# Sparse attention and a softplus layer on one core: values loaded once, fewer small transfers, matmul results in banks of their own

## The chip, the core and the metric

The kernel runs on one core of a Trainium2 chip. A core has five engines that run side by side, each through its own queue in order: TensorE (PE in the profile, its weight loads PEld) multiplies and transposes into PSUM; VectorE (DVE) and ScalarE (ACT) read PSUM and SBUF; GpSimd (POOL) works on SBUF alone; SyncE (SP) issues all the DMAs here. PSUM has eight banks of 512 float32 columns for each of 128 partitions. The metric is the device time of one execution in microseconds: the median of three runs before is 1411.3 us (1410.25 to 1415.76).

## What is computed

```python
def _attn_ref(q, k, v, tau):                      # 8 batches, 8 heads, 576 rows, 64 wide
    scores = 1/sqrt(64) * matmul(q, k^T)
    thresh = max(scores, axis=-1) - tau
    scores = where(scores >= thresh, scores, -1e9)
    attn = exp(scores - max(scores))
    attn = attn / (sum(attn) + 1e-9)
    return matmul(attn, v)

def _moe_ref(x, w_in, w_out):                     # x: 4608 x 512, w_in: 512 x 2048
    h = x @ w_in
    g = maximum(h, 0) + log1p(exp(-abs(h)))       # softplus
    return g @ w_out
```

The attention's output, heads side by side, is x. The output is 4608 x 512 float32.

## The kernel before

**Units and tiles.** A unit is one batch's pair of heads: 8 x 4 = 32 units. Each of the two heads has 576 rows: 512 in four blocks of 128 and a rest of 64. The two rests make one block together, so a unit has nine tiles of 128 query rows: t = 0 to 3 of head 0, t = 4 (`M`) the two rests, t = 5 to 8 of head 1. In SBUF a head's row p x 4 + c lies on partition p in slot c, so that one DMA moves 1 KB runs.

**Per tile.** `scores` multiplies queries by keys into one of two score buffers (`banks`, two PSUM banks each, 288 columns used in each bank). `row_max` (DVE) gives the negated maximum, `exps` (ACT) the exponential into one of three SBUF buffers `e_all` and the threshold, `mask` (DVE) zeroes what lies under the threshold and sums the row. `scores` of tile g + 3 are asked for while tile g is at hand, so they wait for the mask of tile g + 1, which is the last to read that score buffer.

**Whole and split units.** The first eight units (`s.whole`, 72 tiles) keep float32: `whole_T` transposes the exponentials on TensorE, four blocks of 128 into a general PSUM bank (`tm`) and the 64 rest columns into free columns of the tile's score buffer (line 501); ACT copies both (`whole_copy`). The other 24 units split weights and values into float16 halves: `weights_hi` (POOL) writes the upper half of 2^15 e, `weights_lo` (DVE) subtracts it for the lower one, both laid out in nine blocks of 64 columns where upper and lower alternate; a DMA transpose brings them to `eT`, and `values` multiplies nine 128-row blocks of it by the values in `vt`. As each block holds 64 keys' upper halves and the same 64 keys' lower halves, the values of these 64 keys lie on both halves of the partitions: `load_v` loads all values of a split unit twice, with six DMAs. `top_v` finds the largest magnitude of the values for a scale: a DVE maximum per partition, a TensorE product that spreads it over 128 columns into free columns of score buffer 0 (`spare[0]`, line 363), and two points later a maximum over these. `split_v` scales on ACT and splits on POOL, one head at tile 6 and one at tile 8 of the unit before.

**Row scales.** At the end of a unit the reciprocals of the row sums are transposed by TensorE into `spare[1]` (line 595), copied by ACT (`rt`), stored to DRAM (`r_d`), and read back, spread over 64 partitions for each head, by four DMAs into `R` (lines 608 and 609). POOL multiplies the unit's result `xp` by R (line 614); the rest columns then go to DRAM (`x_d`, line 620).

**Queries.** `qkT` transposes keys and queries into general banks; `queries` scales the queries into `qT0` and `swap` writes `qT1`, the same with the two 64-partition halves exchanged, by two DMAs (lines 429 and 430). The block of the two rests, `qm`, is swapped by two more.

**Second layer.** Ten chunks (eight batches' main rows, two sets of rests) go through `hidden` (line 695), `softplus`, the split into `g` (lines 175 and 176) and `project` (line 759). They are interleaved with the attention's tiles by a quota per tile; what is left is done after the last tile.

**Order.** The program is written in the order of the string `PAT`, thirteen different steps per tile with two calls of `point`, and `defer(n, f)` puts f at the n-th point from there. The Tile framework then orders each engine's queue and adds the semaphores; it orders any two accesses of different engines to one PSUM bank. Four general banks (`ps_g`, `GB = 4`) hold transposes, hidden sums, projections and attention results. All helpers' DVE and ACT work shows line 152.

Of the kernel before, what the change touches and what calls it, by code (L numbers as in the profile page):

```python
# [24 lines left out]
P = 128  # L25
# [37 lines left out]
def tile_kernel(ctx: ExitStack, tc: tile.TileContext, q, k, v, tau, w_in, w_out, out):  # L63
# [56 lines left out]
    qm = cpool.tile([P, 2, 2, P], F32R, name="qm")  # L120
# [215 lines left out]
    def load_v(s):  # L336

        if s.whole:
            s.vn = apool.tile([P, 10, D], F32, tag="vt", bufs=2, name=f"vn_{s.i}")
            load_rows(s, s.vn, v)  # L340
            for j in range(2):
                nc.sync.dma_start(
                    s.vn.rearrange("p (h s) d -> p h s d", h=2)[j * SR:(j + 1) * SR, :, NC, :],
                    v[s.b, 2 * s.hp:2 * s.hp + 2, SM:S, :].rearrange("h p d -> p h d"),
                )
            return
        s.vn = apool.tile([P, 2, 9, D], F32, tag="vn", bufs=1, name=f"vn_{s.i}")
        for i in range(2):
            for j in range(2):
                src = v[s.b, 2 * s.hp + j]  # L350
                nc.sync.dma_start(
                    s.vn[i * SR:(i + 1) * SR, j, 1:9, :].rearrange("p (n c) d -> p n (c d)", n=2),
                    src[0:SM, :].rearrange("(n p c) d -> p n (c d)", n=2, c=NC))
            nc.sync.dma_start(s.vn[i * SR:(i + 1) * SR, :, 0, :],
                              v[s.b, 2 * s.hp:2 * s.hp + 2, SM:S, :].rearrange("h p d -> p h d"))

    def top_v(s):
        tops = cpool.tile([P, 1], F32, tag="vtop", bufs=2, name=f"vtop_{s.i}")
        vn = s.vn.rearrange("p s d -> p (s d)" if s.whole else "p h s d -> p (h s d)")
        vec.tensor_reduce(tops, vn, axis=AX.X, op=ALU.max, apply_absolute_value=True)  # L360

        def spread():
            nc.tensor.matmul(spare[0], tops.to_broadcast([P, P]), ident, start=True, stop=True)
            defer(2, take)

        def take():
            top = cpool.tile([P, 1], F32, tag="top", bufs=3, name=f"topv_{s.i}")
            vec.reduce_max(top, spare[0], axis=AX.X)
            to_scale(v_scale[:, s.i:s.i + 1], top)
            ready.add(("v", s.i))  # L370
# [3 lines left out]
    def split_v(s, j):  # L374
        if s.whole:
            return
# [20 lines left out]
    def qkT(s, j, n):  # L397
# [12 lines left out]
        if n == 0:  # L410
            s.kT.append(apool.tile([P, S], F32R, tag="kT", name=f"kT_{s.i}_{j}"))
            t = s.kT[j]
            defer(1, lambda: act.copy(t[:, SR:S], ps))
        else:
            t = [apool.tile([P, SM], F32R, tag=f"qT{i}", name=f"qT{i}_{s.i}_{j}") for i in range(2)]
            s.qT.append(t)
            defer(1, lambda: queries(s, t[0], t[1], ps))

    def queries(s, t0, t1, ps):

        act.activation(t0, ps, AF.Copy, scale=qscale)
        if s.i:
            swap(t0, t1)
# [8 lines left out]
    def qkT_rest(s, j, ps):  # L432

        act.copy(s.kT[j][:, 0:SR], ps[:, j * SR:(j + 1) * SR])
        if j == 0:
# [3 lines left out]
            swap(qm[:, 0], qm[:, 1])  # L439
# [5 lines left out]
    spare = [bank[:, 0, HS:HS + P] for bank in banks]  # L445
    nth = [0]

    def scores(s, t):
        if t == 0:
            s.sums = apool.tile([P, 9], F32, tag="sums", name=f"sums_{s.i}")  # L450
            s.e, s.sp, s.m, s.e16, s.eT, s.bank = {}, {}, {}, {}, {}, {}
# [4 lines left out]
        s.bank[t] = sp  # L456
# [41 lines left out]
    def whole_T(s, t):  # L498
        e = s.e.pop(t)
        main = ps_g.tile([P, NC, P], F32, tag="g", name=f"tm_{s.i}_{t}")  # L500
        rest = s.bank.pop(t)[0:SR, 1, HS:HS + P]
        for c in range(NC):
            nc.tensor.transpose(main[:, c, :], e[:, SR + c * P:SR + (c + 1) * P], ident)
        nc.tensor.transpose(rest, e[:, 0:SR], ident)
# [38 lines left out]
    def weights_hi(s, t):  # L543

        pool, tag, bufs = (apool, "e16", EB) if now["tile"] < TE or t % 2 else (wpool, "wi", WB)
        s.e16[t] = h = pool.tile([P, 9, 2, SR], F16, tag=tag, bufs=bufs, name=f"e16_{s.i}_{t}")
        nc.gpsimd.tensor_scalar(out=h[:, :, 0, :], in0=s.e[t].rearrange("p (c n) -> p c n", n=SR),  # L547
                                scalar1=2.0 ** 15, scalar2=1.0, op0=ALU.mult, op1=ALU.mult)

    def weights_lo(s, t):  # L550
        h = s.e16[t]
        vec.scalar_tensor_tensor(out=h[:, :, 1, :], in0=s.e.pop(t).rearrange("p (c n) -> p c n", n=SR),
                                 scalar=2.0 ** 15, in1=h[:, :, 0, :], op0=ALU.mult, op1=ALU.subtract)

    def weights_T(s, t):
# [3 lines left out]
        h = s.e16.pop(t).rearrange("p c i n -> p (c i n)")  # L559
        if t == M:  # L560
            nc.sync.dma_start_transpose(s.eT[0][:, :, SM:S], h[0:SR])
            nc.sync.dma_start_transpose(s.eT[1][:, :, SM:S], h[SR:P])
# [4 lines left out]
    def values(s, g):  # L567
# [4 lines left out]
        for c in range(9):  # L572
            slot = 0 if c == 0 else 1 + 4 * ((c - 1) % 2) + (c - 1) // 2
            nc.tensor.matmul(o[:, 0:HS], s.vt[:, j, slot, :], s.eT[j][:, c, x0:x0 + HS], start=(c == 0), stop=(c == 8))  # L574
# [23 lines left out]
    def row_scales_out(s):  # L598
# [461 lines left out]
```

## Time and profile before

| | us |
|---|---|
| median of three runs | 1411.3 |
| the profiled execution | 1418.82 |
| its span, first to last instruction | 1417.1 |
| PE busy | 1296.0 |
| DVE / ACT / POOL busy | 919.3 / 920.1 / 943.4 |

The profile counts an engine as busy while one of its instructions runs; matmuls overlap each other, so a busy TensorE is not one at its peak. The whole units fill the first 330 us or so, the split units the stretch to about 1277 us (the last transposed block is multiplied at 1276.5 us), and the rest is the second layer alone. A row "A <- B: x, n, y" of the waits reads: engine and tile A stood idle x us in total, n times, at most y us, until B was done. A row of groups has line, engine, operation, tiles, shapes and count, then busy us and the mean ns of one. A row of one tile's or one line's instructions has minimum, median and maximum ns. The timeline gives start, length, engine, line, operation and, in brackets, the idle time before it with what ended it. A row of stretches has length, then busy us and count for PE, PEld, DVE, ACT and POOL, then the granted clock of TensorE, the mean busy share of 16 DMA engines and GB/s.

### The profile page before, as it was taken

What the parts mean: (1) busy time and instruction counts of PE and PEld (TensorE: products, weight loads), DVE (VectorE), ACT (ScalarE), POOL (GpSimd) and SP (SyncE); (2) the same over time, 40 slices, a digit from 0 to 9 for tenths busy, and PEclk for the clock granted to TensorE, in tenths of its full rate; (3) what the DMA queues carried; (4) which work ended last, traced back from release to release, by engine and by line L of the source; (5) the groups of instructions that cost most, each with busy time, mean ns of one, the idle gap of its engine ahead of it and who ended that gap; (6) DMA issues with size and microseconds to landing.
All of it is one profiled execution on the core that took longest, in us unless ns stands there. A gap on an engine that the chain in (4) does not pass through costs nothing.

```text
span 1417.1 us, 22079 instructions
## 1 busy us (share of the span) xinstructions
PE 1296.0 (91%) x7192; PEld 772.2 (54%) x7192; DVE 919.3 (65%) x1695; ACT 920.1 (65%) x1759; POOL 943.4 (67%) x1033
## 2 busy tenths in 40 slices
PE   6988899899898989899889989898999999999998
PEld 4555555455555555555555555555555765554455
DVE  5878765546777767767777777768667776751011
ACT  5867787766576758665776657666876677753222
POOL 2576876737677778668666777778767778646242
PEclk9998999999999999999999999999999999999999
DMA  5534432213766665656656676766565655631010
GB/s 138 158 108 135 123 99 84 67 38 86 152 127 132 132 146 127 133 129 144 133 131 130 122 153 128 136 123 152 118 133 129 144 115 104 112 77 40 0 38 15
DMA packets 351107, 159.19 MB, mean 112 GB/s; under 512 B 294128, under 2 KB 330256, under 8 KB 350992
## 3 DMA queue, kind: packets, MB, share of 16 engines
q1 hardware_dynamic: 350992, 157.78, 50.4%
q8 instruction: 57, 0.93, 0.3%
q14 instruction: 58, 0.48, 0.1%
HBM read 62.92 MB, written 10.63 MB: 52 GB/s over the span
## 4 chain that ended last, share of the span: by engine, by line
PE 41%; POOL 16%; DVE 13%; ACT 12%; DMA 7%; issue 7%; SPq 4%; POOLq 0%; ACTq 0%; DVEq 0%
PE o L759 12%; PE h L695 12%; PE s L464 6%; PE pv L574 4%; ACT st L152 3%; DVE e L152 3%; PE pv L533 3%; ACT L152 3%; DVE e_all L152 3%; DVE negm L152 3%; DMA R<-r_d 2%; ACT e_all L152 2%; POOL g L176 2%; POOL e L547 2%; POOL q L132 2%
## 5 line engine op out<-in xcount | busy, mean ns | idle before, releaser
L759 PE MATMUL o<-w_o,g 128*128 128x512 f16 x1728 | 422.8, 388 | 14.0 <-POOL g L175 9.6
L695 PE MATMUL h<-xh,w_i 128*128 128x512 f16 (+1 forms) x1280 | 364.4, 361 | 1.8 <-DVE xp L152 1.3
L152 ACT ACTIVATE e_all<-s,negm 128x576 f32<-128x576 f32 x288 | 213.1, 740 | 160.5 <-DVE negm L152 154.0
L152 DVE TENSOR_REDUCE negm<-s 128x1 f32<-128x576 f32 x288 | 215.5, 748 | 135.5 <-PE s L464 102.6
L547 POOL TENSOR_SCALAR e<-e_all 128x576 f16<-128x576 f32 x216 | 202.0, 938 | 149.1 <-DVE e_all L152 140.4
L464 PE MATMUL s<-kT,qT 128*128 128x288 f32 x1024 | 226.5, 342 | 69.8 <-DVE e_all L152 38.9
L152 DVE SCALAR_TENSOR_TENSOR e_all<-s,thr,e_all 128x576 f32<-128x576 f32 x288 | 233.1, 809 | 74.7 <-ACT thr L152 27.3
L695 PEld LDWEIGHTS <-w_i 128*128 128x128 f16 x1920 | 180.3, 99 | 164.6 <-issue 11.3
L759 PEld LDWEIGHTS <-g 128*128 128x128 f16 x1728 | 161.1, 100 | 193.6 <-POOL g L175 16.3
L152 DVE SCALAR_TENSOR_TENSOR e<-e_all,e 128x576 f16<-128x576 f32 x216 | 217.0, 1005 | 36.7 <-POOL e L547 36.6
L695 PE MATMUL h<-xl,w_i 128*128 128x512 f16 (+1 forms) x640 | 231.5, 362 | 2.4 <-POOL xl L176 2.4
L464 PEld LDWEIGHTS s<-kT,qT 128*128 128x128 f32 x1024 | 162.0, 197 | 116.8 <-DVE e_all L152 62.1
L152 DVE SCALAR_TENSOR_TENSOR acc<-o,c,acc 128x512 f32<-128x512 f32 x108 | 80.3, 744 | 181.9 <-PE o L759 121.0
L176 POOL TENSOR_TENSOR g<-st,g 128x512 f16<-128x512 f32 x144 | 168.9, 1177 | 7.5
L175 POOL TENSOR_SCALAR g<-st 128x512 f16<-128x512 f32 x144 | 92.1, 644 | 106.6 <-ACT st L152 106.0
L152 ACT ACT_TABLE_LOAD x119 | 152.7, 1283 | 14.6 <-PE h L695 6.7
L152 ACT ACTIVATE st<-h,c 128x512 f32<-128x512 f32 x144 | 91.1, 683 | 69.2 <-PE h L695 68.4
L574 PE MATMUL pv<-eT,vt 128*128 128x288 f16 x864 | 131.9, 292 | 0.2
L152 ACT COPY xp<-pv 64x288 f32<-64x288 f32 (+3 forms) x136 | 50.8, 378 | 112.1 <-PE pv L574 102.0
L533 PE MATMUL pv<-gw,vn 128*64 128x256 f32 (+3 forms) x320 | 101.2, 437 | 0.0
L614 POOL TENSOR_TENSOR xp<-xp,R 128x576 f32<-128x576 f32 x32 | 46.8, 1463 | 80.8 <-DMA R<-r_d 65.6
L574 PEld LDWEIGHTS <-vt 128*128 128x128 f16 x864 | 79.9, 100 | 34.9 <-issue 2.2
(104 smaller groups left out, 1658.5 us busy)
## 6 DMA issues: line engine op xcount, KB each, us to landing
qT<-qT SPq DMA_DIRECT2D x124, 128.0 KB
vn<-in_v_dram SPq DMA_DIRECT2D x96, 128.0 KB
kn<-in_k_dram SPq DMA_DIRECT2D x32, 256.0 KB
qn<-in_q_dram SPq DMA_DIRECT2D x32, 256.0 KB
wc_i<-in_moe_w_in_dram SPq DMA_DIRECT2D x16, 512.0 KB
R<-r_d SPq DMA_DIRECT2D x64, 128.0 KB
wc_o<-in_moe_w_out_dram SPq DMA_DIRECT2D x16, 512.0 KB
out_dram<-acc SPq DMA_DIRECT2D x32, 256.0 KB
```

The lines of the kernel that those rows point to most:

```text
L132: eng.tensor_tensor(out=out_, in0=in_, in1=hi.bitcast(F32), op=ALU.subtract)
L152: i = getattr(self.eng, name)(*args, **kwargs)
L175: nc.gpsimd.tensor_scalar(out=hi, in0=x, scalar1=1.0, scalar2=1.0, op0=ALU.mult, op1=ALU.mult)
L176: nc.gpsimd.tensor_tensor(out=lo, in0=x, in1=hi, op=ALU.subtract)
L464: nc.tensor.matmul(sp[:, hf, 0:HS], lhs, s.kT[j][:, hf * HS:(hf + 1) * HS], start=(m == 0), stop=(m == len(parts) - 1))
L533: nc.tensor.matmul(o[0:D, 0:n], s.vn[k_, 5 * j + c, :], h[k_, c, 0:n], start=(c == 0), stop=(c == NC))
L547: nc.gpsimd.tensor_scalar(out=h[:, :, 0, :], in0=s.e[t].rearrange("p (c n) -> p c n", n=SR), scalar1=2.0 ** 15, scalar2=1.0, op0=ALU.mult, ...
L574: nc.tensor.matmul(o[:, 0:HS], s.vt[:, j, slot, :], s.eT[j][:, c, x0:x0 + HS], start=(c == 0), stop=(c == 8))
L614: nc.gpsimd.tensor_tensor(out=s.xp, in0=s.xp, in1=s.R, op=ALU.mult)
L695: nc.tensor.matmul(bank[:, i * u.T:(i + 1) * u.T], wi[g, cc][:, a, e], x[cc], start=(cc == 0 and m == 0), stop=(cc == NCC - 1 and m == 2))
L759: nc.tensor.matmul(o, u.g[fc][m // 2][:, sl], wo[fc][:, m % 2, :], start=(n == 0), stop=(n == 3 * QF - 1))
```

## The change

- **Values once.** The weights of a tile are laid out as 576 upper halves, then the lower halves of the last 64 keys, then those of the first 512. After the transposition block c < 4 holds the upper halves of 128 keys, block 4 the upper and the lower halves of the last 64, blocks 5 to 8 the lower halves. Only the last 64 values are needed on both halves of the partitions; the rest is loaded once, by three DMAs, in the layout of the whole units. `split_v` is one step of 640 columns per unit, at tile 7 of the unit before. The keys move from columns 64 to 575 to columns 0 to 511. `weights_lo` becomes two instructions, of 512 and 64 columns.
- **Fewer transfers.** The rests of k and q are loaded by one DMA each, R by two, results of two tiles are stored by one; the queries of head 0 and the block of rests lie in one tile `q0`, swapped together.
- **Banks.** The spread top, the transposed row scales and the transposed rest of whole units go to general banks; the top is taken one point after its product.
- **The ring of g at the end** has ten pairs of buffers where it had eleven, as the tags of the queries hold one buffer each.

```diff
+    q0 = cpool.tile([P, 2, SM + 2 * P], F32R, name="q0")
+    qm = q0[:, :, SM:].rearrange("p n (m c) -> p n m c", m=2)
...
     def natural(s, src, name):
-        for j in range(2):
-            nc.sync.dma_start(t[j * SR:(j + 1) * SR, NC, :], src[s.b, 2 * s.hp + j, SM:S, :])
+        nc.sync.dma_start(t[:, NC, :], src[s.b, 2 * s.hp:2 * s.hp + 2, SM:S, :])
...
     def load_v(s):
+        s.vn = apool.tile([P, 10, D], F32, tag="vt" if s.whole else "vn", bufs=2 if s.whole else 1, name=f"vn_{s.i}")
+        load_rows(s, s.vn, v)
         for i in range(2):
-            for j in range(2):
-                src = v[s.b, 2 * s.hp + j]
-                nc.sync.dma_start(
-                    s.vn[i * SR:(i + 1) * SR, j, 1:9, :].rearrange("p (n c) d -> p n (c d)", n=2),
-                    src[0:SM, :].rearrange("(n p c) d -> p n (c d)", n=2, c=NC))
-            nc.sync.dma_start(s.vn[i * SR:(i + 1) * SR, :, 0, :],
-                              v[s.b, 2 * s.hp:2 * s.hp + 2, SM:S, :].rearrange("h p d -> p h d"))
+            nc.sync.dma_start(
+                s.vn.rearrange("p (h s) d -> p h s d", h=2)[i * SR:(i + 1) * SR, :, NC, :],
+                v[s.b, 2 * s.hp:2 * s.hp + 2, SM:S, :].rearrange("h p d -> p h d"),
+            )
...
         def spread():
-            nc.tensor.matmul(spare[0], tops.to_broadcast([P, P]), ident, start=True, stop=True)
-            defer(2, take)
+            ps = ps_g.tile([P, 512], F32, tag="g", name=f"topv_{s.i}")
+            nc.tensor.matmul(ps[:, 0:P], tops.to_broadcast([P, P]), ident, start=True, stop=True)
+            defer(1, lambda: take(ps))
...
-    def split_v(s, j):
-        if s.whole:
-            return
-        if j == 0:
-            s.vt = apool.tile([P, 2, 9, 2 * D], F16, tag="vt", bufs=2, name=f"vt_{s.i}")
-        vj = s.vn[:, j]
-        act.activation(vj, vj, AF.Copy, scale=v_scale[:, s.i:s.i + 1])
-        halves(s.vt[:, j, :, 0:D], s.vt[:, j, :, D:2 * D], vj)
+    def split_v(s):
+        s.vt = apool.tile([P, 10, 2 * D], F16, tag="vt", bufs=2, name=f"vt_{s.i}")
+        act.activation(s.vn, s.vn, AF.Copy, scale=v_scale[:, s.i:s.i + 1])
+        halves(s.vt[:, :, 0:D], s.vt[:, :, D:2 * D], s.vn)
...
+            if j == 0:
+                t = [q0[:, i, 0:SM] for i in range(2)]
+            else:
+                t = [apool.tile([P, SM], F32R, tag=f"qT{i}", bufs=1, name=f"qT{i}_{s.i}") for i in range(2)]
...
         if s.i:
-            swap(t0, t1)
+            if j == 0:
+                swap(q0[:, 0], q0[:, 1])
+            else:
+                swap(t0, t1)
...
-            swap(qm[:, 0], qm[:, 1])
+            if s.i == 0:
+                swap(qm[:, 0], qm[:, 1])
...
-        rest = s.bank.pop(t)[0:SR, 1, HS:HS + P]
+        rest = ps_g.tile([P, NC, P], F32, tag="g", name=f"tr_{s.i}_{t}")[0:SR, 0, :]
...
-        s.e16[t] = h = pool.tile([P, 9, 2, SR], F16, tag=tag, bufs=bufs, name=f"e16_{s.i}_{t}")
-        nc.gpsimd.tensor_scalar(out=h[:, :, 0, :], in0=s.e[t].rearrange("p (c n) -> p c n", n=SR),
-                                scalar1=2.0 ** 15, scalar2=1.0, op0=ALU.mult, op1=ALU.mult)
+        s.e16[t] = h = pool.tile([P, 2 * S], F16, tag=tag, bufs=bufs, name=f"e16_{s.i}_{t}")
+        nc.gpsimd.tensor_scalar(out=h[:, 0:S], in0=s.e[t], scalar1=2.0 ** 15, scalar2=1.0, op0=ALU.mult, op1=ALU.mult)
...
     def weights_lo(s, t):
-        h = s.e16[t]
-        vec.scalar_tensor_tensor(out=h[:, :, 1, :], in0=s.e.pop(t).rearrange("p (c n) -> p c n", n=SR),
-                                 scalar=2.0 ** 15, in1=h[:, :, 0, :], op0=ALU.mult, op1=ALU.subtract)
+        h, e = s.e16[t], s.e.pop(t)
+        for i, o in ((slice(0, SM), slice(S + SR, 2 * S)), (slice(SM, S), slice(S, S + SR))):
+            vec.scalar_tensor_tensor(out=h[:, o], in0=e[:, i], scalar=2.0 ** 15, in1=h[:, i],
+                                     op0=ALU.mult, op1=ALU.subtract)
...
+        order = (0, 5, 1, 6, 2, 7, 3, 8, 4)
+        for n, c in enumerate(order):
+            nc.tensor.matmul(o[:, 0:HS], s.vt[:, 5 * j + (c if c <= NC else c - NC - 1), :],
+                             s.eT[j][:, c, x0:x0 + HS], start=(n == 0), stop=(n == 8))
...
     def row_scales_T(s):
-        nc.tensor.transpose(spare[1][0:9], s.rs, ident)
-        defer(1, lambda: row_scales_out(s))
+        ps = ps_g.tile([P, 512], F32, tag="g", name=f"rT_{s.i}")
+        nc.tensor.transpose(ps[0:9, 0:P], s.rs, ident)
+        defer(1, lambda: row_scales_out(s, ps))
...
     def load_R(s):
-        for j in range(2):
-            nc.sync.dma_start(s.R[j * D:(j + 1) * D, 0:SM], rows[j * SM:(j + 1) * SM].partition_broadcast(D))
-            nc.sync.dma_start(s.R[j * D:(j + 1) * D, SM:S],
-                              rows[2 * SM + j * SR:2 * SM + (j + 1) * SR].partition_broadcast(D))
+        for a, n in ((0, SM), (2 * SM, SR)):
+            nc.sync.dma_start(s.R[:, a and SM:(a and SM) + n],
+                              rows[a:a + 2 * n].rearrange("(j n) -> j n", j=2)[:, None, :].to_broadcast([2, D, n]))
...
-            spare = [("kT", 2), ("qT0", 2), ("qT1", 2), ("nat", 2), ("e16", EB)]
+            spare = [("kT", "kT", 2), ("qT0", "qT1", 1), ("nat", "nat", 2), ("e16", "e16", EB)]
...
     def store_out(u, tb, a):
         if u.main:
-            dst = out[u.b * S:u.b * S + SM, :].rearrange("(p c) e -> p c e", c=NC)[:, tb, :]
-            nc.sync.dma_start(dst, a)
+            dst = out[u.b * S:u.b * S + SM, :].rearrange("(p c) e -> p c e", c=NC)
+            if u.tail:
+                nc.sync.dma_start(dst[:, tb, :], a)
+            elif tb % 2:
+                nc.sync.dma_start(dst[:, tb - 1:tb + 1, :], u.pairs[tb // 2])
...
-            times = ((s.i - 1, 0), (s.i - 1, 3), (s.i - 1, 6), (s.i - 1, 8))
-        for at_, f in zip(times, (load_v, top_v, lambda x: split_v(x, 0), lambda x: split_v(x, 1))):
+            times = ((s.i - 1, 0), (s.i - 1, 3), (s.i - 1, 7))
+        for at_, f in zip(times, (load_v, top_v, split_v)):
```

More of the change, by code (lines that the diff above doesn't have):

```diff
@@ L412, in qkT, with queries @@
             t = s.kT[j]
-            defer(1, lambda: act.copy(t[:, SR:S], ps))
+            defer(1, lambda: act.copy(t[:, 0:SM], ps))
         else:
-            t = [apool.tile([P, SM], F32R, tag=f"qT{i}", name=f"qT{i}_{s.i}_{j}") for i in range(2)]
+            if j == 0:
+                t = [q0[:, i, 0:SM] for i in range(2)]
+            else:
+                t = [apool.tile([P, SM], F32R, tag=f"qT{i}", bufs=1, name=f"qT{i}_{s.i}") for i in range(2)]
             s.qT.append(t)
-            defer(1, lambda: queries(s, t[0], t[1], ps))
-    def queries(s, t0, t1, ps):
+            defer(1, lambda: queries(s, j, t[0], t[1], ps))
+    def queries(s, j, t0, t1, ps):
         act.activation(t0, ps, AF.Copy, scale=qscale)
         if s.i:
-            swap(t0, t1)
+            if j == 0:
+                swap(q0[:, 0], q0[:, 1])
+            else:
+                swap(t0, t1)
             return
@@ L432, in qkT_rest @@
     def qkT_rest(s, j, ps):
-        act.copy(s.kT[j][:, 0:SR], ps[:, j * SR:(j + 1) * SR])
+        act.copy(s.kT[j][:, SM:S], ps[:, j * SR:(j + 1) * SR])
         if j == 0:
@@ L455, in scores @@
         s.sp[t] = sp
-        s.bank[t] = sp
         if t == M:
```

45 lines of the change are left out of this document (15 added, 30 removed).

## The prediction

> **What bounds the kernel now.** I read the stretches by stage first, then what TensorE waits for, then single episodes in the timeline. One execution is profiled: 1418.82 us, of which the span is 1417.1 us, 7.5 us above the median of 1411.3 us; the sum is made on that execution and its difference then put on the median.
>
> ```profile
> 30.00:180.00 150.00, 128.14 (x683) 82.57 (x681) 120.59 (x248) 110.34 (x276) 104.93 (x111) 0.93 0.46 128
> 180.00:330.00 150.00, 144.48 (x758) 82.08 (x756) 83.19 (x171) 113.63 (x237) 95.11 (x106) 0.99 0.25 68
> 400.00:1000.00 600.00, 541.48 (x3037) 323.90 (x3037) 442.33 (x790) 400.81 (x733) 433.94 (x469) 0.97 0.65 134
> 1000.00:1250.00 250.00, 242.29 (x1450) 149.91 (x1449) 173.97 (x314) 179.30 (x315) 181.86 (x198) 0.99 0.58 122
> core 0: 1417.1 us, clock 0.973
> PE 1296.0 (91%) x7192; PEld 772.2 (54%) x7192; DVE 919.3 (65%) x1695; ACT 920.1 (65%) x1759; POOL 943.4 (67%) x1033
> ```
>
> The columns are the length, then the busy time of PE, PEld, DVE, ACT and POOL, the granted clock, DMA share and GB/s. PE is the bound: 1296.0 of 1417.1 us, so 121 us idle at most to win, and 2.7% of the clock (38 us). The idle time lies from 30 to 180 us (21.9 us) and from 400 to 1000 us (58.5 us); after 1000 us PE is 97% busy. So only those two stages can pay.
>
> ```profile
> PE s L464 <- DVE e_all L152: 39.6, 32, 5.2
> PE s L464 <- DMA qT<-qT: 15.8, 12, 2.2
> PE s L464 <- DVE topv L152: 14.2, 6, 3.7
> PE s L504 <- ACT e_all L152: 12.9, 11, 3.1
> PE o L759 <- POOL g L175: 9.6, 9, 2.2
> POOL xp L614 <- DMA R<-r_d: 65.6, 17, 7.2
> DVE negm L152 <- ACT rt L152: 31.5, 12, 4.4
> DVE e_all L152 <- ACT gw L152: 23.7, 20, 3.3
> DVE e_all L152 <- PE s L363: 12.4, 8, 2.1
> PE tr L409 <- ACT gw L152: 0.6, 2, 0.4
> ```
>
> Each row has us in total, times, longest. Scores wait for the mask that frees their bank (39.6), for swapped queries (15.8), for the values' top, which lies in a score bank (14.2); the short transposes of whole units wait for an exponential that reads the bank they share (12.9). The R wait is POOL's, and one step from PE.
>
> **The change, part by part.** *Results in own banks.* The rows "topv", "L504", "rt", "gw" and "L363" are waits of one bank's users for each other; they go. What is late next is seen in one episode.
>
> ```profile
> 501.93 1.41 POOL L614 TENSOR_TENSOR xp<-xp,R 128x576 f32<-128x576 f32 x1 [1.64 <-DMA R<-r_d]
> 507.01 1.15 DVE L152 SCALAR_TENSOR_TENSOR e<-e_all,e 128x576 f16<-128x576 f32 x1 [3.28 <-POOL e L547]
> 508.09 0.28 DVE L152 TENSOR_REDUCE topv<-s 128x1 f32<-128x128 f32 x1
> 508.42 1.33 PE L464 MATMUL s<-kT,qT 128*128 128x288 f32 x4 [3.66 <-DVE topv L152]
> 602.46 1.47 PE L759 MATMUL o<-w_o,g 128*128 128x512 f16 x6
> 510.46 0.81 DVE L152 SCALAR_TENSOR_TENSOR e_all<-s,thr,e_all 128x576 f32<-128x576 f32 x1
> L152 DVE TENSOR_REDUCE negm<-s 128x1 f32<-128x576 f32 x288 | 215.5, 748 | 135.5 <-PE s L464 102.6 <-ACT rt L152 31.5
> ```
>
> PE stood from 504.76 to 508.42. Without the shared bank it runs these scores, some transposes and six projections (1.47 us where the clock is full) and then needs the mask that now ends at 511.27. That mask stays behind the DVE's work of 507.01, which waited for POOL, which had waited for R; at best the maximum and the mask follow 508.16 directly and end at 509.7 (748 + 810 ns). So 1.5 of 3.66 us stay won: two fifths. I take two fifths for every wait removed, an estimate from this episode.
>
> The top is taken one point (half a tile) sooner. If the DVE comes before PE there, it waits with maxima and masks behind it and PE behind them; the L363 row (12.4 us in 8) is what such waits cost today, and as I count only part of that row as won, nothing more is charged.
>
> *Swaps.* The queries of half 0 and the masked block share a tile: six transfers per unit become four.
>
> ```profile
> 622.97 0.49 SPq L429 DMA_DIRECT2D qm<-qm  x1
> 623.85 0.48 SPq L430 DMA_DIRECT2D qm<-qm  x1
> 624.43 0.55 SPq L429 DMA_DIRECT2D qT<-qT  x1
> 781.39 0.82 PE L464 MATMUL s<-kT,qT 128*128 128x288 f32 x2 [2.05 <-DMA qT<-qT]
> 780.70:787.60 6.90, 6.21 (x21) 3.38 (x22) 3.44 (x6) 3.26 (x7) 6.07 (x8) 0.51 0.65 130
> 787.60:794.50 6.90, 6.90 (x41) 4.11 (x40) 5.83 (x14) 3.11 (x7) 5.69 (x7) 1.00 0.45 86
> ```
>
> The queries go out 1.46 us sooner (624.43 - 622.97), more than the mean wait of 1.3 us (15.8/12); rows grow from 2 to 3 KB, which takes some of it back. The masked block is read four tiles later, so tying it to the queries costs nothing. After the 2.05 us gap PE runs at half clock: 21 matmuls, then 41, in equal stretches. So waits cost twice. The Trainium skill, "TensorE: Matmul & The Clock Gate" (Part 1), has the clock fall after an idle window of some 3.4 us; here 2.05 us did it, so the trace does not agree, and by the page's rule the clock term below would be near zero.
>
> *Values once, R in two, other merges.* Per later unit the values take 3 issues for 6, R 2 for 4, k and q 2 for 3 each: SP issues nine fewer with the swaps. POOL and ACT split 640 columns once where they split 576 twice, at a tile between the two of before; the top is reduced over 640, not 1152. The lower halves become two instructions.
>
> ```profile
> L176 POOL TENSOR_TENSOR vt<-vn,vt 128x576 f16<-128x576 f32 x48 | 62.1, 1293 | 1.3
> L175 POOL TENSOR_SCALAR vt<-vn 128x576 f16<-128x576 f32 x48 | 36.1, 752 | 1.7 <-ACT vn L152 1.6
> L152 DVE TENSOR_REDUCE vtop<-vn 128x1 f32<-128x1152 f32 x24 | 32.4, 1349 | 2.4 <-DMA vn<-in_v_dram 1.0 <-DMA r_d<-rt 1.0
> L152 DVE TENSOR_REDUCE vtop<-vn 128x1 f32<-128x640 f32 x8 | 6.5, 813 | 1.5 <-DMA vn<-in_v_dram 1.5
> L152 DVE SCALAR_TENSOR_TENSOR e<-e_all,e x216: 743/758/1946, 330.0 to 1266.3; 128x576 f16<-128x576 f32 x108
> L152 DVE TENSOR_REDUCE topv<-s x32: 275/278/292, 29.3 to 1218.0; 128x1 f32<-128x128 f32 x32
> L152 DVE TENSOR_SCALAR topv<-topv x32: 136/153/155, 30.3 to 1218.3; 128x1 f32<-128x1 f32 x32
> L608 SPq DMA_DIRECT2D R<-r_d x64: 452/578/603, 56.9 to 1277.4; - x64
> L609 SPq DMA_DIRECT2D R<-r_d x64: 577/592/653, 57.4 to 1278.0; - x64
> L152 ACT COPY gw<-tm 128x512 f32<-128x512 f32 x64 | 37.2, 581 | 15.1 <-PE tm L503 14.8
> 0.00:30.00 30.00, 16.44 (x79) 13.51 (x80) 15.98 (x30) 15.36 (x34) 6.89 (x15) 1.00 0.54 148
> ```
>
> POOL: 2 x (752 + 1293) ns = 4.1 us becomes about 2.3 us (640/576 once), 1.8 us less in each of 24 units; it shortens the queue behind R, of which "POOL g" shows 9.6 us at PE. DVE lower halves: 512 columns lie between 674 ns (758 x 512/576) and 758 ns, 64 columns between 153 and 278 ns; together 827 to 1036 for 758. I take 920, as a line from 153 at one column to 758 at 576 gives 690 + 220: 0.16 us x 216 = 35 us more DVE, less 24 x 0.54 = 13 us of shorter reduces: 22 us. The mask on the same queue frees the banks, so I charge a third, 7 us; the bounds are 0 and 22.
>
> R: two issues fewer send it off 1.17 us sooner (578 + 592 ns); twice the bytes in each lands later. At the stage's 134 GB/s 256 KB take 1.0 us more than 128 KB, so I take nothing; the bad end is the third rival.
>
> PSUM: 72 rests, 32 tops and 32 row scales become 136 more users of the four general banks. PE waits for those banks' readers hardly at all (0.6 us in the row "tr"), the lower bound is 0, and less where a result is read sooner; were each to hold PE up for one copy of 581 ns it would be 79 us. From 180 to 330 us the hidden, value and transposed results are all there at once, so I take a tenth, 8 us. Merged stores, the ring one pair shorter at the end and the values' new order touch no wait shown: 0 (stores lie beside PE; cover gone, half a us each).
>
> **Sum.** Waits removed: 14.2 + 12.9 + 15.8 + 9.6 = 52.5 us, and a quarter of 39.6 for the DVE's rt, gw and L363 waits: 62.4 us; two fifths is 25 us. Clock: 38 us x 52.5/121 = 16 us, two fifths is 6 us. Against it 7 + 8 = 15 us. Net 16 us: the profiled 1418.8 to 1403, on the median 1411.3 to **1395 us**. Own range 1380 to 1407.
>
> **Rivals.**
> 1. *The waits do not come back.* Three quarters are kept: 47 + 12 - 15 = 44 us, 1367 us. For it: POOL's and DVE's relief in the same units. Against: the episode above.
> 2. *No change, 1411 us.* The chain R, POOL, lower halves, mask sets the pace of a unit, and PE's gaps only move. For it: 65.6 us of R waits stay.
> 3. *R becomes slower, and the kernel with it.* The new source of R counts first over the two heads and then 64 equal rows. If the transfer is dealt out by that first count, two DMA engines carry 128 KB each and one 16 KB more. In the first 30 us an engine moves 148/(16 x 0.54) = 17 GB/s, so 8.5 us for 1.1 on sixteen: R lands up to 6 us later. POOL's R waits average 3.9 us (65.6/17); taking the longest, 7.2, to stand behind the longest "POOL g" wait, 2.2, some 5 us are covered, 1.1 are left, and the smaller split gives 1.8. Of 6 us, 3 reach PE, of 4 us 1: at 2.2 in 17 units 38 us more, less the 16: 1433 us. It decides from R landing about 4 us later than now. For it: R is late now already; against: no row shows a transfer so dealt out.
>
> The Trainium skill, "DMA: Bandwidth & Descriptors" (Rules for kernel authors), says an outermost count below 16, a leading broadcast for one, confines a transfer to that many engines. By that page's 435 GB/s for sixteen, one engine would need 4.8 us for 128 KB. No run here shows it.
>
> 4. *Banks run out* from 30 to 330 us, 30 us instead of 8: 1417 us.
>
> **Chances.** Forecast 0.33, rival 1 0.14, rival 2 0.14, rival 3 0.34, rival 4 0.05. Both signs hold much, so the range goes from 1368 (leaving half of rival 1) to 1437 us. A measurement tells 0.5% (7 us) from no change. Faster: the forecast but its edge (0.31), rival 1 (0.14) and 0.03 of rival 3, together 0.48. Within 0.5%: rival 2, most of rival 4 and edges of the forecast and rival 3, 0.20. Slower: the rest, 0.32.
>
> **What would show it.** Right: the topv, rt and L504 rows gone, "PE s <- DVE e_all" above 39.6 us, the qT row below 8 us, POOL's vt near 2.3 us per unit, the lower halves at two pieces of some 0.92 us together. Rival 3: "POOL xp <- DMA R" above 100 us instead of near 50. Rival 4: PE idle above 6 us from 180 to 330 us. Wrong above all if the compiler's order of POOL's queue around R differs, since all the rest waits behind it.

## The result, and the profile after

The changed kernel takes 1516.2 us (median of four runs, 1513.2 to 1520.8), the kernel before 1413.4 us in the same session: 1.072 times the time, 95% interval 1.070 to 1.075. The forecast was 1395, its range 1368 to 1437: the time lies beyond the range, on the slower side, and 83 us beyond the rival of that side. Of the page of the changed kernel the span, the busy times and the chain that ended last by line:

```profile
span 1515.3 us, 21809 instructions
...
PE 1326.3 (88%) x7192; PEld 784.1 (52%) x7192; DVE 990.6 (65%) x1911; ACT 903.0 (60%) x1735; POOL 886.5 (59%) x985
...
PE o L750 11%; DMA R<-r_d 9%; PE h L686 9%; PE s L454 6%; DVE e L153 5%; DVE e_all L153 4%; PE pv L564 4%; DMA q<-q 4%; DVE negm L153 3%; ACT st L153 3%; ACT L153 3%; PE pv L523 3%; POOL g L177 2%; POOL xp L605 2%; DVE acc L153 1%
```

PE stands idle for 189 us (1515.3 - 1326.3) where it stood 121, and the same 7192 instructions take 30 us more, as the clock is lower (0.942 for 0.973): 68 + 30 is the 98 us by which the span grew. In the chain that ended last R's transfer holds 9% of the span, some 136 us, where it held 2%. The stretches (columns as in the prediction) place the loss:

```profile
30.00:180.00 150.00, 126.79 (x640) 80.12 (x639) 108.68 (x231) 102.25 (x263) 97.99 (x104) 0.89 0.44 123
180.00:330.00 150.00, 137.32 (x720) 77.99 (x720) 82.81 (x169) 107.62 (x225) 87.72 (x98) 0.99 0.24 72
400.00:1000.00 600.00, 505.44 (x2743) 300.45 (x2742) 439.19 (x835) 354.65 (x649) 357.03 (x394) 0.92 0.64 113
```

From 30 to 330 us PE is 8.5 us less busy than before (264.1 for 272.6); from 400 to 1000 us it does 2743 matmuls where it did 3037, at a clock of 0.92 for 0.97. From 30 to 330 us it does 1360 matmuls where it did 1441. So most of the loss lies in the split units. The waits say behind what:

```profile
POOL xp L605 <- DMA R<-r_d: 145.0, 26, 14.8
...
PE s L454 <- DMA q<-q: 48.1, 17, 4.9
...
PE s L454 <- DVE e_all L153: 46.4, 35, 5.0
...
PE o L750 <- POOL g L177: 30.1, 20, 5.0
PE o L750 <- POOL g L176: 25.8, 26, 5.8
```

The rows for the shared score banks are gone, as meant. But POOL waits 145.0 us for R (65.6 before), PE 48.1 us for swapped queries (15.8) and 55.9 us for g (12.4 in the same two rows). One episode of the timeline shows how these hang together:

```profile
615.74 1.10 SPq L600 DMA_DIRECT2D R<-r_d  x2
...
618.10 5.30 SPq L555 DMA_TRANSPOSE eT<-e  x1
...
622.11 1.10 ACT L153 ACTIVATE q<-tr,qscale 128x64 fp32r<-128x64 f32 x3
...
624.45 1.41 POOL L605 TENSOR_TENSOR xp<-xp,R 128x576 f32<-128x576 f32 x1 [6.49 <-DMA R<-r_d]
...
625.82 0.68 POOL L537 TENSOR_SCALAR e<-e_all 128x576 f16<-128x576 f32 x1
...
625.89 0.35 SPq L611 DMA_DIRECT2D x_d<-xp  x1
...
626.46 0.41 POOL L126 TENSOR_SCALAR q<-qn 128x256 fp32r<-128x256 f32 x1
...
627.79 2.54 SPq L552 DMA_TRANSPOSE eT<-e  x2
...
628.63 0.60 PE L750 MATMUL o<-w_o,g 128*128 128x512 f16 x2 [0.80 <-POOL g L176]
...
631.68 0.54 SPq L420 DMA_DIRECT2D q<-q  x1
632.27 0.59 SPq L421 DMA_DIRECT2D q<-q  x1
...
635.82 0.85 PE L454 MATMUL s<-kT,q 128*128 128x288 f32 x2 [4.49 <-DMA q<-q]
```

R is issued at 615.74 and its product starts 8.7 us later. Two queues stand still in between. POOL's does for 6.49 us, and behind the product stand the upper halves of the next tile, the split of the other head's queries and g, for which PE waits. SP's does for 5.30 us in a transpose (the longest of these took 2.42 us before), and then until the product is done: next in SP's queue stands the store of the product's rest columns (`x_d`, 625.89), and behind it a load, two transposes, two more loads and the swap. The queries of this swap were scaled by 623.2 (ACT), but it goes out at 631.68 and lands 3 us after the end of its last issue: PE stands 4.49 us. SP's waits for that store over the whole run, in the changed kernel and before:

```profile
SPq L611 <- POOL xp L605: 103.4, 30, 9.8
```

```profile
SPq L620 <- POOL xp L614: 45.7, 20, 4.4
```

### The profile page after: what moved, and what is told of

The parts are those of the page before. It is cut to its first block, busy times and chain, and to the rows that moved or that the text cites. A ratio compares the mean times of both kernels' runs of the same rounds, so it can differ in the third digit from the quotient of the medians.

```text
span 1515.3 us, 21809 instructions
## 1 busy us (share of the span) xinstructions
PE 1326.3 (88%) x7192; PEld 784.1 (52%) x7192; DVE 990.6 (65%) x1911; ACT 903.0 (60%) x1735; POOL 886.5 (59%) x985
## 4 chain that ended last, share of the span: by engine, by line
PE 35%; DVE 18%; DMA 16%; POOL 10%; ACT 10%; issue 7%; SPq 4%; POOLq 0%; DVEq 0%; ACTq 0%
PE o L750 11%; DMA R<-r_d 9%; PE h L686 9%; PE s L454 6%; DVE e L153 5%; DVE e_all L153 4%; PE pv L564 4%; DMA q<-q 4%; DVE negm L153 3%; ACT st L153 3%; ACT L153 3%; PE pv L523 3%; POOL g L177 2%; POOL xp L605 2%; DVE acc L153 1%
## 5 line engine op out<-in xcount | busy, mean ns | idle before, releaser
L750 PE MATMUL o<-w_o,g 128*128 128x512 f16 x1728 | 432.5, 392 | 57.0 <-POOL g L177 30.1
L153 DVE SCALAR_TENSOR_TENSOR e<-e_all,e 128x512 f16<-128x512 f32 (+1 forms) x432 | 298.0, 730 | 49.1 <-POOL e L537 49.1
L153 DVE SCALAR_TENSOR_TENSOR e_all<-s,thr,e_all 128x576 f32<-128x576 f32 x288 | 233.0, 809 | 48.4 <-ACT thr L153 47.6
L454 PE MATMUL s<-kT,q 128*128 128x288 f32 x768 | 166.1, 343 | 89.6 <-DMA q<-q 48.1
L454 PEld LDWEIGHTS s<-kT,q 128*128 128x128 f32 x768 | 121.8, 201 | 130.2 <-DVE e_all L153 61.8
L605 POOL TENSOR_TENSOR xp<-xp,R 128x576 f32<-128x576 f32 x32 | 45.0, 1406 | 180.0 <-DMA R<-r_d 145.0
L176 POOL TENSOR_SCALAR g<-st 128x512 f16<-128x512 f32 x144 | 96.1, 669 | 91.3 <-ACT st L153 91.1
L564 PE MATMUL pv<-eT,vt 128*128 128x288 f16 x864 | 138.9, 306 | 0.9 <-DVE xp L153 0.5
L454 PE MATMUL s<-kT,qT 128*128 128x288 f32 x512 | 112.8, 343 | 9.1 <-DVE e_all L153 8.9
```

The source lines that it names most:

```text
L153: i = getattr(self.eng, name)(*args, **kwargs)
L176: nc.gpsimd.tensor_scalar(out=hi, in0=x, scalar1=1.0, scalar2=1.0, op0=ALU.mult, op1=ALU.mult)
L454: nc.tensor.matmul(sp[:, hf, 0:HS], lhs, s.kT[j][:, hf * HS:(hf + 1) * HS], start=(m == 0), stop=(m == len(parts) - 1))
L564: nc.tensor.matmul(o[:, 0:HS], s.vt[:, 5 * j + (c if c <= NC else c - NC - 1), :], s.eT[j][:, c, x0:x0 + HS], start=(n == 0), stop=(n == 8))
L605: nc.gpsimd.tensor_tensor(out=s.xp, in0=s.xp, in1=s.R, op=ALU.mult)
L750: nc.tensor.matmul(o, u.g[fc][m // 2][:, sl], wo[fc][:, m % 2, :], start=(n == 0), stop=(n == 3 * QF - 1))
```

## The experiments

Each time is beside the kernel before in the same session (1414.6, 1415.2, 1414.6 and 1416.1 us in the four sessions), with the ratio's 95% interval. Three theories stood against each other at the start: R's loads, dealt out over two DMA engines; the lower halves in two pieces and the banks; the rests of k and q, which have the same form as R.

**Is it R? The changed kernel with R as before (e1), and with the rests as before too (e2).**

```diff
-        for a, n in ((0, SM), (2 * SM, SR)):
-            nc.sync.dma_start(s.R[:, a and SM:(a and SM) + n],
-                              rows[a:a + 2 * n].rearrange("(j n) -> j n", j=2)[:, None, :].to_broadcast([2, D, n]))
+        for j in range(2):
+            nc.sync.dma_start(s.R[j * D:(j + 1) * D, 0:SM], rows[j * SM:(j + 1) * SM].partition_broadcast(D))
+            nc.sync.dma_start(s.R[j * D:(j + 1) * D, SM:S],
+                              rows[2 * SM + j * SR:2 * SM + (j + 1) * SR].partition_broadcast(D))
...
-        nc.sync.dma_start(t[:, NC, :], src[s.b, 2 * s.hp:2 * s.hp + 2, SM:S, :])
+        for j in range(2):
+            nc.sync.dma_start(t[j * SR:(j + 1) * SR, NC, :], src[s.b, 2 * s.hp + j, SM:S, :])
```

> The changed kernel with only R's loads put back to four DMAs of 64 equal rows each. Theory (R dealt out over two DMA engines): R lands again some 2 to 3 us after its last issue, the row POOL xp <- DMA R falls from 145.0 to below 70 us, the transposes behind it on SP no longer hold for 5 us, and the time falls from 1516 by 80 to 110 us, to 1405 to 1435. Rival (two-piece lower halves and the results in general banks cost it): R waits fall too, but the time stays above 1480, with DVE topv <- PE and POOL e <- DVE e_all as now. Rival (the rests of k and q, also one source count of two, hold SP and the queries): above 1450.

> As the first of these, with the rests of k and q loaded by two DMAs each again. R theory alone: within 5 us of the first, since 32 KB on two engines in a load that is not waited for is hidden. Rival (rests): at least 15 us faster than the first, and the wait for swapped queries (48.1 us) falls in this one and not in the first.

e1: 1413.8 us (0.9995, 0.997 to 1.002). e2: 1399.7 us (0.9897, 0.9872 to 0.9921). R is worth 102.4 us (1516.2 - 1413.8), the rests 14.1 behind it. The waits of e1, then of e2:

```profile
POOL xp L606 <- DMA R<-r_d: 60.4, 17, 12.9
...
PE s L454 <- DMA q<-q: 33.2, 18, 3.4
```

```profile
POOL xp L607 <- DMA R<-r_d: 48.4, 14, 12.3
...
PE s L455 <- DMA q<-q: 19.7, 18, 1.8
```

R's row is back where it was; with the rests undone the wait for queries falls as often, but by 13.5 us. The rests' 14 us were in neither expectation (5 at most, or 15 at least); e13 and e14 go on with them.

**Is it R alone, and is it the engines? The kernel before with R as changed (e3), and with R in four loads whose 64 equal rows are counted as 4 x 16 (e4).**

```diff
-            nc.sync.dma_start(s.R[j * D:(j + 1) * D, 0:SM], rows[j * SM:(j + 1) * SM].partition_broadcast(D))
+            nc.sync.dma_start(s.R[j * D:(j + 1) * D, 0:SM],
+                              rows[j * SM:(j + 1) * SM][None, None, :].to_broadcast([4, 16, SM]))
```

> The kernel before with only R's loads in the changed form, two DMAs whose source counts first over two heads. R theory: 1490 to 1515, POOL xp <- DMA R from 65.6 to above 130, PE waits for swapped queries from 15.8 to above 30. Rival (the rest of the change costs it): 1411 to 1440, since R's wait is POOL's and mostly covered.

> A dose: the kernel before with R's four loads, the 64 equal rows counted as 4 times 16, so that four engines would carry 64 KB each and 8 KB more. R theory: R lands some 2 us later than before, half of what two engines add, POOL xp <- DMA R between 80 and 120, and the time between 1430 and 1470. If the number of descriptors or the form of the broadcast were the cause and not the engines: as before, 1411.

e3: 1529.2 us (1.0812, 1.0792 to 1.0832), 115 us more than before, with nothing else changed, and 14 above the upper bound given. POOL's wait for R is 211.2 us there, as expected, but PE's wait for swapped queries is 10.9 us, below the 15.8 of before and not above 30: with six swaps the loss shows as PE's wait for g (94.9 us in the two rows that had 12.4). e4: 1441.1 us (1.0203, 1.0174 to 1.0231), 26 more, with POOL's wait for R at 121.1 us. e4 moves the same bytes in the same four loads to the same rows; only the way the equal rows are counted differs. One unit each, R's first issue and the product that waits for it, of before, of e4 and of the changed kernel:

```profile
423.22 0.54 SPq L608 DMA_DIRECT2D R<-r_d  x1
...
428.25 1.41 POOL L614 TENSOR_TENSOR xp<-xp,R 128x576 f32<-128x576 f32 x1 [7.21 <-DMA R<-r_d]
```

```profile
423.68 0.58 SPq L608 DMA_DIRECT2D R<-r_d  x1
...
429.78 1.40 POOL L614 TENSOR_TENSOR xp<-xp,R 128x576 f32<-128x576 f32 x1 [8.43 <-DMA R<-r_d]
```

```profile
403.87 1.11 SPq L600 DMA_DIRECT2D R<-r_d  x2
405.18 6.51 SPq L555 DMA_TRANSPOSE eT<-e  x1
...
412.75 1.42 POOL L605 TENSOR_TENSOR xp<-xp,R 128x576 f32<-128x576 f32 x1 [7.70 <-DMA R<-r_d]
```

From issue to product: 5.0, 6.1 and 8.9 us in these units; over all 24 split units the medians are 5.0, 6.6 and 8.8. Outermost counts of 64, 4 and 2 give that order. The packets in the traces show it more directly: R's large loads are packets of 2 KB that take 84 ns in the median in all three kernels, and the first 64 of them start within 1.0 us before, 1.5 in e4 and 2.8 in the changed kernel (medians of split units). By an estimate from these numbers (64 x 84 ns over each time) that is more than five, some four and two under way at a time. The Trainium skill, "DMA: Bandwidth & Descriptors" (Rules for kernel authors), has a transfer confined to as many engines as an outermost count below 16 allows; by that, 16, 4 and 2. The traces agree, in the order and in the dose. In time, 1.6 us later in the median costs 26 us and 3.8 us later 102 to 115. Put on the 24 split units that is 1.1 and 4.3 to 4.8 us a unit, and on all 32, as the whole units lose some of it, 0.8 and 3.2 to 3.6 (both estimates): most of the delay arrives at TensorE.

**By which way? The product later (e5, e6); the product further back in POOL's queue (e9, e12); a two-engine load that nobody waits for (e10).**

```diff
-XD = 8
+XD = 10
```

> The changed kernel, R as changed, but POOL's product with R asked for one tile later (10 points behind R's loads instead of 8). If R's delay reaches TensorE through POOL, whose queue stands still behind the product: POOL xp <- DMA R falls from 145.0 to below 40 us and the time from 1516 to 1405 to 1440. If it reaches TensorE through SP and the DMA engines (transposes and swaps held behind a transfer on two engines): R's wait at POOL falls as well, but the SP transposes behind R still take above 5 us and the time stays above 1480. Between: both.

> The changed kernel with R's four loads and the rests' two (1399.7 us) and the product with R one tile later. If the 48.4 us in which POOL still waits for R are on the path as R's other 4 us per unit were: 1360 to 1385. If POOL has slack of its own at 2 us: 1395 to 1405. It can also lose where the next layer's x is then late: above 1405.

e5 is the changed kernel with that edit, e6 is e2 with it. e5: 1518.7 us (1.0738, 1.0707 to 1.077); e6: 1397.5 (0.9886, 0.9858 to 0.9913); each is where it came from. As experiments both failed: in e5 the scheduler left the product at the same place in POOL's queue, between the upper halves of the same two tiles, and R's wait stayed (136.9 us for 145.0, in e6 45.5 for 48.4). So in e9 a dependence puts it two tiles further back, behind the upper halves asked for last:

```diff
+        his.append(nc.gpsimd.tensor_scalar(out=h[:, 0:S], ...))
...
-        nc.gpsimd.tensor_tensor(out=s.xp, in0=s.xp, in1=s.R, op=ALU.mult)
+        behind(nc.gpsimd.tensor_tensor(out=s.xp, in0=s.xp, in1=s.R, op=ALU.mult), his)
```

> The changed kernel, R as changed, with POOL's product with R tied behind the upper halves that were asked for last, so that it stands two tiles further back in POOL's queue (asking for it later had left it where it was). If R's delay reaches TensorE through POOL, whose queue stands still behind the product: POOL xp <- DMA R from 145.0 to below 40 us and the time from 1516 to 1400 to 1440. If through SP and the DMA engines, where transposes and swaps are held behind a transfer on two engines: R's wait at POOL goes and the time stays above 1480, the transposes behind R still at 5 us. Between: both, and the difference from 1516 is POOL's share.

e10 is e2 with one more load behind R's four:

```diff
+        dump = dpool.tile([P, SM], F32, name=f"dump{s.i}")
+        nc.sync.dma_start(dump, rows[0:2 * SM].rearrange("(j n) -> j n", j=2)[:, None, :].to_broadcast([2, D, SM]))
```

> The other side of that: the changed kernel with R's four loads and the rests' two (1399.7 us), and behind R one more load of the changed form (256 KB, its source counted first over two heads) to a place in DRAM that nobody reads. POOL does not wait for it. If POOL's wait is the cause: 1400 to 1415, for one issue of 0.55 us more on SP per unit. If transposes and swaps held behind two busy DMA engines are the cause: above 1470, SP's transpose behind it above 5 us and the wait for swapped queries above 30 us.

e9: 1443.7 us (1.0198, 1.0163 to 1.0234); e10: 1449.4 (1.0239, 1.0218 to 1.026). Between, both times. The waits of e9, its SP queue, and the waits of e10:

```profile
POOL xp L607 <- DMA R<-r_d: 34.8, 6, 15.5
...
PE s L454 <- DMA q<-q: 32.5, 16, 4.8
```

```profile
592.52 1.10 SPq L602 DMA_DIRECT2D R<-r_d  x2
594.56 5.62 SPq L557 DMA_TRANSPOSE eT<-e  x1
```

```profile
PE s L455 <- DMA q<-q: 53.7, 20, 6.4
...
POOL xp L609 <- DMA R<-r_d: 48.7, 14, 11.3
```

With POOL's wait for R down from 145.0 to 34.8 us, 72.5 of the 102.4 us go (1516.2 - 1443.7), while SP's transpose still takes 5.62 us. With the load alone and POOL's wait as in e2 (48.7 against 48.4), 49.7 us come (1449.4 - 1399.7), and the wait for swapped queries grows from 19.7 to 53.7 us; SP's longest transpose is 3.93 us there, not above 5. So there are two ways, and they overlap: **POOL's queue**, in order behind a late product, and **the DMA queue**, where transposes and swaps stand behind two busy engines. SP's queue is part of the first way too, through the store of the product: its wait there falls from 103.4 to 52.7 us in e9. Whether transposes or swaps matter more on the second way was not tried, and neither was a load of the same size on sixteen engines beside e10: how much of its 49.7 us belongs to the two engines and how much to one more load stays open.

**What are the other parts worth? Six swaps (e7), own banks alone (e8), values once alone (e11).** e7 is e2 with the queries' and the rests' swaps apart (and, with their tiles, eleven pairs in the ring of g again); e8 and e11 are the kernel before with one part each (e11 with the merged stores).

```diff
-    q0 = cpool.tile([P, 2, SM + 2 * P], F32R, name="q0")
+    qm = cpool.tile([P, 2, 2, P], F32R, name="qm")
...
-            if j == 0:
-                swap(q0[:, 0], q0[:, 1])
-            else:
-                swap(t0, t1)
+            swap(t0, t1)
...
```

> The changed kernel with R's four loads and the rests' two, and six swaps per unit again (queries and the block of rests apart). My working took a gain from the queries going out 1.46 us sooner: by it some 5 to 10 us slower than 1399.7 and the wait for swapped queries above its 19.7 us. Rival (rows of 3 KB and the tile with one buffer eat it): 1390 to 1400, with a shorter wait for queries.

> The kernel before with the three results (spread top, transposed row scales, short transposes of whole units) in general banks, the top taken one point after its product, and nothing else of the change. My working: 25 us kept of the waits less 8 for the general banks, with the share of the clock: 1390 to 1403; the rows topv, L504, rt gone, a new row DVE topv <- PE topv. Rival (the waits only move): 1408 to 1420.

> The kernel before with the values loaded once and their layout, the single split and the merged stores, and without the banks, swaps, R's and the rests' merges. Own banks alone gave 1412.9 and all but R, rests and swaps 1394.2. If the gain of 20 us is the values': 1390 to 1400. If it comes only when both are there (the banks' waits, once gone, need POOL's relief to pay): 1405 to 1415. My working charged this part with 7 us for the DVE and gave it 9.6 us of waits for g.

e7: 1394.2 us (0.9869, 0.9837 to 0.9901); e8: 1412.9 (0.9991, 0.9969 to 1.0013); e11: 1409.6 (0.9976, 0.9954 to 0.9998). Own banks alone bring 2 us, which the interval does not separate from nothing, values once 5, just clear of it, and the two together, in e7, some 20. The waits of e8 show where those of the banks went:

```profile
POOL xp L616 <- DMA R<-r_d: 67.3, 13, 12.7
PE s L465 <- DVE e_all L152: 46.3, 29, 5.3
...
PE s L465 <- DMA qT<-qT: 27.4, 13, 3.3
```

The rows of the shared banks (14.2 and 12.9 us at PE) are gone; in their place the mask (39.6) and the queries (15.8) are waited for by 6.7 and 11.6 us more. R's wait is as before. So two thirds of the wait (18.3 of 27.1 us) moved down the chain.

**The rests and the swaps (e13, e14), and R's wait before the change (e15).** e13 is before with the rests in one load each, e14 is e7 with that, e15 is before with the product further back as in e9.

> The kernel before with only the rests of k and q in one DMA each, source counted first over two heads. Rests on two engines cost by themselves: 1422 to 1432, the wait for swapped queries above its 15.8 us. Rival (they cost only where the merged swap of 3 KB rows stands behind them, or nothing, as my working had it): 1408 to 1418.

> The version with six swaps (1394.2 us), with the rests of k and q in one DMA each. Rests on two engines cost by themselves: 1402 to 1412. Rival (only with merged swaps, where they cost 14 us): 1391 to 1398.

> The kernel before with only POOL's product with R tied behind the upper halves asked for last. If R's wait of 65.6 us bounded a unit there: 1370 to 1400, and the gain of the other parts was held back by it. If POOL's and DVE's queues bound it (values twice, shared banks): 1403 to 1416, with PE's rows for shared banks as they were, and the gain of 16 us seen on the changed version needs its relief.

e13: 1415.2 us (0.9993, 0.9977 to 1.001); e14: 1395.4 (0.9854, 0.9833 to 0.9875). With six swaps the merged rests cost nothing; with merged swaps they cost 14 us (e1 against e2). Put the other way, with merged rests the merged swaps (with the shorter ring) cost 18 us (1413.8 - 1395.4), and without them 5.5, which the intervals of e2 and e7 do not separate. In e1 the rests' load stands right ahead of the swap; the last swap's issue and the scores that need it, in e1 and in e2:

```profile
427.93 0.59 SPq L421 DMA_DIRECT2D q<-q  x1
...
432.18 0.50 PE L454 MATMUL s<-kT,q 128*128 128x288 f32 x2 [2.64 <-DMA q<-q]
```

```profile
424.93 0.59 SPq L422 DMA_DIRECT2D q<-q  x1
...
428.36 0.50 PE L455 MATMUL s<-kT,q 128*128 128x288 f32 x2 [1.74 <-DMA q<-q]
```

3.7 us from the end of the issue in the one, 2.8 in the other, in one unit each. That the rests' rows on two engines are what stands ahead was not shown by itself; e2 also has the swap ahead of the second load.

e15: 1391.2 us (0.983, 0.9814 to 0.9846). R's wait falls from 65.6 to 10.0 us, and the time by 25:

```profile
POOL xp L616 <- DMA R<-r_d: 10.0, 2, 9.2
```

So R's wait at POOL, with all that stands behind it, bounded a split unit before anything was changed. SP's wait for the store of the product falls with it (45.7 to 16.3 us), and so does PE's wait for swapped queries (15.8 to 4.0).

**A version that beats both (e12):** e7 with the product further back.

> The version with six swaps (1394.2 us) and the product with R two tiles further back in POOL's queue. If R's 2 us still cost a unit what R's other 4 us do: 1350 to 1380, with the row POOL xp <- DMA R (51.5) near 0. If POOL has slack for them: 1390 to 1398.

e12: 1378.5 us, 0.9742 of before (0.9721 to 0.9763); R's 51.5 us of waits at POOL fall to 4.3, and the time by 16 (1394.2 - 1378.5). SP's wait for the store falls from 79.4 us in e7 to 25.9, PE's for swapped queries from 14.6 to 0.3. The rows of e12, and its stretch from 400 to 1000 us:

```profile
SPq L607 <- POOL xp L601: 25.9, 8, 7.1
...
PE s L447 <- DMA qT<-qT: 0.3, 1, 0.3
```

```profile
400.00:1000.00 600.00, 559.45 (x3224) 335.73 (x3222) 533.88 (x978) 416.33 (x761) 432.17 (x459) 0.99 0.65 133
```

3224 matmuls in 600 us where before did 3037 and the changed kernel 2743; the clock is 0.99, where it was 0.97 and 0.92. So much of the wait for swapped queries hung on when the product was done. The episode above shows it in SP's queue; SP's share and that of the queries' own split on POOL were not tried apart.

## Why the prediction was wrong

**The step that failed: R, taken at nothing in the sum.** Its bad end stood in the third rival, with the mechanism that the runs bear out (the source counts first over two heads, so two engines carry it), but priced at 38 us where it is 102. Not the delay was mis-sized: up to 6 us were allowed and 3.8 measured. The cover was. The prediction had POOL hide 5 us of R's wait, as the longest wait for g at PE was 2.2 us where R's was 7.2; with the smaller split 2.9 us of that were to be left, so that 1 to 3 us in 17 units were charged. But PE does not meet that queue in g alone. Behind the product stand the upper halves, without which there is no lower half and, behind it in DVE's queue, no mask and no free bank; the next split of queries; and, in SP's queue, the store of the product with the next transposes and swaps behind it. Measured were 0.8 to 1.1 us a unit for 1.6 us of delay (e4) and 3.2 to 4.8 for 3.8 (e1, e3), so little or no cover; e15 shows that it was already used up before. The second way, transposes and swaps behind the two engines (up to 49.7 us alone), was in no part of the prediction. The rival's sign, R's wait above 100 us, came (145.0). The compiler's order of POOL's queue around R, which the prediction named as its weakest point, did differ: between R's issue and the product stands one upper half in 23 of 24 split units, where it was one in 9 and none in 14. That is not what cost the time: e3 has the order of before and loses 115 us, e1 has the new order and loses nothing.

**Swaps: the sign was wrong.** The queries' wait was to fall below 8 us. It was 48.1 us in the changed kernel, and 19.7 in e2 where e7, with six swaps, has 14.6. Merged swaps cost 18 us beside merged rests; "rows grow from 2 to 3 KB, which takes some of it back" named the loss and did not price it. The rests, at nothing, are right only where the swaps are apart.

**Results in own banks: the waits went, the time did not.** The topv, L504 and rt rows are gone and the mask's row rose above 39.6, both as forecast, but two fifths of 62.4 us, all the removed waits together, were to stay won. Alone the banks gave 2 us (e8). This is the second rival's mechanism, R's chain setting the pace and PE's gaps moving, as e15 bears out; the episode that gave the two fifths was read without asking what the next unit waits for. The fourth rival's sign, more than 6 us idle from 180 to 330 us, is there, as e8's stretches show, but not its loss:

```profile
30.00:180.00 150.00, 132.62 (x709) 83.21 (x708) 119.19 (x255) 113.17 (x285) 110.46 (x117) 0.97 0.46 132
180.00:330.00 150.00, 140.25 (x732) 78.56 (x731) 80.74 (x158) 107.56 (x225) 94.79 (x104) 0.99 0.25 68
```

From 180 to 330 us PE does 732 matmuls where it did 758, and stands idle for 9.8 us (5.5 before); but from 30 to 180 us it does 709 where it did 683. Over both stretches it is 1441 in either kernel, with 27.1 us idle for 27.4.

**Values once.** POOL's split came out as worked out, 0.74 + 1.42 us per unit in the changed kernel:

```profile
L177 POOL TENSOR_TENSOR vt<-vn,vt 128x640 f16<-128x640 f32 x24 | 34.1, 1419 | 1.2
L176 POOL TENSOR_SCALAR vt<-vn 128x640 f16<-128x640 f32 x24 | 17.8, 742 | 0.8 <-ACT vn L153 0.8
```

The lower halves did not: 298.0 us of DVE in the page's group of both pieces, which overlap a little, is 1.38 us per tile, where 0.92 was taken, and the start was 1.00 and not 0.76, since the median was used where the mean counts. DVE's busy time rose by 71 us (990.6 - 919.3) and not by 22. It cost little: e7, with all of it, is the fastest of the versions that leave the product in place.

**The rest of the sum had the right sign.** It gave 16 us, some 8 of them without the swaps' share (two fifths of 15.8 us of waits, and of the clock that goes with them); e7, which holds just banks, values and stores, has some 20. But its parts were not what the sum had: alone they bring 2 and 5, and the rest comes only with both. That the whole sum of 16 us lies close to the 20 of e7 is luck.

**The clock.** The sense was right: 68 us more of idle time came with 30 us more of busy time. The episode was read loosely, though. The trace has the clock lowered at 780.73 us, 1.4 us into the gap of 2.05 us and after two shorter ones (0.63 and 0.20 us), so the long gap alone did not do it.

## What to carry to other kernels

Before two transfers are merged, compare the outermost counts of both sides before and after: here two loads that count first over 2 were slower than four that count first over 64, and held up what was queued behind them. An engine's wait for a transfer is covered only if nothing in that engine's queue behind the waiting instruction is on the path; follow each instruction behind it, not the one that shows a row, and each other queue that waits for one of them, as SP's did for the store. A removed wait pays only where the next wait of the same unit is not already as late, so parts that bring little alone can bring more together.

## What the runs showed of the hardware that was not expected

A small DVE instruction can take as long as a POOL instruction beside it. The pieces of the lower halves in the changed kernel, by form, and the range of both:

```profile
L153 DVE SCALAR_TENSOR_TENSOR e<-e_all,e 128x512 f16<-128x512 f32 x216 | 177.1, 820 | 49.1 <-POOL e L537 49.1
L153 DVE SCALAR_TENSOR_TENSOR e<-e_all,e 128x64 f16<-128x64 f32 x216 | 138.2, 640 | 0.0
```

```profile
L153 DVE SCALAR_TENSOR_TENSOR e<-e_all,e x432: 211/685/1940, 344.6 to 1365.8; 128x512 f16<-128x512 f32 x72, 128x64 f16<-128x64 f32 x72
```

64 columns take 211 ns at best and 640 in the mean, close to the 0.68 us of POOL's upper halves in the timeline. In the trace 27 of the 216 small pieces ran while no POOL instruction did, and took 211 to 220 ns; the 189 others took 700 ns in the mean. The Trainium skill, "SBUF — State Buffer" (SBUF: two separate sides), says that a DVE instruction with two SBUF inputs and a GpSimd instruction that reads SBUF exclude each other for a whole instruction. The trace agrees with that; no run took POOL's instruction away, so the cause is not shown by an experiment.

And a two-engine transfer reaches further than its reader: SP's transposes, 1.3 us in the median, took up to 6.51 us when they were issued behind R in the changed kernel, and at most 2.42 before.
